# Loading every second chunk of Q with an outer dimension of 8 in a grouped-query attention kernel

## The chip, the cores and the metric

The kernel runs on one core of a Trainium2 chip. The metric is the device time of one execution in microseconds (us). "PE" is the matrix engine, "DVE" the vector engine, "ACT" the scalar engine, "POOL" the GpSimd engine and "SP" the sync engine, which issues nearly all DMA transfers here. A transfer from memory (HBM) into on-chip memory (SBUF, 128 partitions) is moved in packets (37349 in the kernel before) by sixteen DMA engines side by side: each K load shows sixteen arrivals, near 20 us within 0.44 us. Profiles are of one execution; times are medians of several executions without the profiler. Kernels are compared only within the same rounds.

## The reference

```python
B, Hq, Hkv, Sq, Sk, D = 16, 32, 8, 16, 2048, 128      # all bfloat16

def reference(q, k, v):
    k = jnp.repeat(k, Hq // Hkv, axis=1)               # four query heads share one K/V head
    v = jnp.repeat(v, Hq // Hkv, axis=1)
    scores = jnp.einsum("bhqd,bhkd->bhqk", q, k) * D ** -0.5
    p = softmax(scores, axis=-1)
    return jnp.einsum("bhqk,bhkd->bhqd", p, v)
```

K and V hold 67 MB each and are read once; Q and the output hold 2.1 MB each. In the profile, 136.3 MB are read from memory and 2.1 MB written.

## The kernel before

One queue (SP) loads K and V in pieces of 1 MB into a ring of fifteen buffers ("slots"), and Q in eight chunks of 1024 rows, 256 KB each. A slot is loaded again as soon as the work that read it is done. Each chunk of Q is rearranged on POOL (the first on DVE and ACT), transposed on PE, and read out of PSUM in the right row order by ACT or DVE. A Q row has 256 bytes; NI is 8, so a partition gets eight neighbouring rows.

```python
for t in range(NP + LAG):                 # order of issue on the one queue
    if t < NP:             dma.append(("K", t))
    if qstep.get(t, 0):    dma.append(("Q", qstep[t]))
    if t >= LAG:           dma += v_of(t - LAG)
    ...                                   # and the output stores

# the load of chunk x of Q: partition a gets rows 8a to 8a+7
dst, src = Qn[x % 2][:, :, :], qf[qch * x:qch * (x + 1), :].rearrange("(a i) d -> a i d", i=NI)
sp.dma_start(dst, src).then_inc(*prog_sem(prog, op))        # its semaphore counts to 16

# "qt": eight transposes of 128 x 128, one for each i
for i in range(NI):
    pe.transpose(QT_ps[:, 128 * i:128 * (i + 1)], Qr[:, x, i, :], ident[:, :])

# "qe": the PSUM read, which puts the rows back into order
dst = QT[p % 2][:, op[2], :].rearrange("d (a i) -> d a i", i=NI)
src = QT_ps[:, 0:qch].rearrange("d (i a) -> d a i", i=NI)
```

A 1 MB load of K or V fills all 128 partitions with 8 KB each, K in packets of 8 KB and V (all but its last, halved piece) in packets of 4 KB. An output store reads 64 partitions.

Of the kernel before, what the change touches and what calls it, by code (L numbers as in the profile page):

```python
# [210 lines left out]
def bass_standalone__gqa_softmax__sampling_kernel(  # L211
# [14 lines left out]
    qch = min(QCH, NROWS)  # L226
    assert NROWS % qch == 0 and qch % 128 == 0
    NI = qch // 128
# [8 lines left out]
    Qn = [sb(f"Qn{i}", [128, NI, 128], BF16) for i in range(2)]  # L237
    Qr = sb("Qr", [128, 4, NI, 128], BF16)
    QT = [sb(f"QT{i}", [128, 4, qch], BF16) for i in range(2)]
# [19 lines left out]
    QT_ps = ps("QT_ps", [128, 1024], BF16)  # L259
# [58 lines left out]
    qf = q.rearrange("b h s d -> (b h s) d")  # L318
# [6 lines left out]
    def mark_hint(eng, me, prog, op):  # L325

        if not prog.general and op == prog.progs[me][max(0, len(prog.progs[me]) - HINT[me])]:
            hints[me] = eng.mark_branch_hint_location()

    def o_tile(p):  # L330
        return Osb[(p // 2 if p < NP - 1 else NP // 2) % NBO][:, p % 2, :]

    def out_rows(p, gg):

        g = group_of(p, gg)
        return of[64 * g:64 * (g + 1), :], o_tile(p)[64 * gg:64 * (gg + 1), :]

    def prog_sem(prog, op):
        return prog.point(op)[0], 16

    def group_of(p, gg):
        return 4 * (p // 2) + 2 * gg + p % 2

    def elementwise(eng, me, prog, before_last=None):
        waits = prog.waiter(eng, me)
        for op in prog.progs[me]:
            kind, p = op[0], op[1]
            if before_last is not None and op == prog.progs[me][-1]:
                before_last()
            waits(op)  # L350
            mark_hint(eng, me, prog, op)
            if kind == "kx":
                _, _, gg, h = op
                ins = eng.transpose(KT[p % NKT][:, gg, :, h],  # L354
                                    prog.slot(("K", 2 * p + gg))[:, J * 64 * h:J * 64 * (h + 1)])
            elif kind == "qr":
                x = op[2]
                dst = Qr[:, x, :, :].rearrange("m i (a d) -> m i a d", a=4)
                src = bass.AP(Qn[p % 2], (x // 2) * 64 + x % 2, [[NI * 128, 128], [128, NI], [0, 4], [2, 32]])
                ins = eng.activation(dst, src, ACT.Copy) if me == "act" else eng.tensor_copy(dst, src)  # L360
            elif kind == "mx":
                h, part = op[2], slice(Sk // 2 * (p % 2), Sk // 2 * (p % 2 + 1))
                ins = eng.tensor_scalar(Sneg[p % 2][:, Sk // 2 * h:Sk // 2 * (h + 1)], S_ps[:, part], -scale, None,
                                        op0=ALU.mult, op1=ALU.min, accum_out=nhalf[:, p, h:h + 1])
            elif kind == "nb":
                ins = eng.tensor_tensor(nbias[:, p:p + 1], nhalf[:, p, 0:1], nhalf[:, p, 1:2], op=ALU.min)
            elif kind == "ex":
                h = op[2]
                if prog.general:
                    src = Sneg[p % 2][:, Sk // 2 * h:Sk // 2 * (h + 1)]  # L370
                else:
                    src = S_ps[:, Sk // 2 * (p % 2):Sk // 2 * (p % 2 + 1)]
                ins = eng.activation(  # L373
                    P[p % 2][:, :].rearrange("m (r a h j) -> m h a r j", h=2, a=2, j=32)[:, h],
                    src.rearrange("m (a r j) -> m a r j", a=2, j=32), ACT.Exp,
                    bias=nbias[:, p:p + 1] if prog.general else 0.0, scale=-1.0 if prog.general else scale,
                    accum_out=rhalf[:, p, h:h + 1])
            elif kind == "rs":
                ins = eng.tensor_tensor(rowsum[:, p:p + 1], rhalf[:, p, 0:1], rhalf[:, p, 1:2], op=ALU.add)  # L379
            elif kind == "STA":  # L380
                eng.dma_start(*out_rows(NP - 1, 1)).then_inc(*prog_sem(prog, op))
                continue
            elif kind == "rc":
                ins = eng.reciprocal(rrec[:, p:p + 1], rowsum[:, p:p + 1])  # L384
            elif kind == "nm":
                dst, src, r = o_tile(p), O_ps[:, 0:128], rrec[:, p:p + 1]
                if me == "act":
                    ins = eng.activation(dst, src, ACT.Copy, scale=r)  # L388
                else:
                    ins = eng.tensor_scalar(dst, src, r, None, op0=ALU.mult)  # L390
            else:
                if kind == "qe":
                    dst = QT[p % 2][:, op[2], :].rearrange("d (a i) -> d a i", i=NI)
                    src = QT_ps[:, 0:qch].rearrange("d (i a) -> d a i", i=NI)
                else:
                    h = op[2]
                    dst = PT[p % NPT][:, 8 * h:8 * (h + 1), :]
                    src = PT_ps[h][:, :].rearrange("k (t m) -> k t m", t=8)
                ins = eng.activation(dst, src, ACT.Copy) if me == "act" else eng.tensor_copy(dst, src)  # L399
            ins.then_inc(prog.sem_eng[me], 1)  # L400

    def transfers(sp, prog):
        waits = prog.waiter(sp, "sp")
        for op in prog.progs["sp"]:
            kind, x = op
            waits(op)
            mark_hint(sp, "sp", prog, op)
            if kind == "K":
                dst = prog.slot(op)[:, :].bitcast(BF16)
                src = kf[2 * x:2 * x + 2].rearrange("g (b r) d -> (g b) (r d)", r=2 * J)  # L410
            elif kind[0] == "V":
                p, part = (x, slice(0, J)) if kind == "V" else (NP - 1, slice(J // 2 * x, J // 2 * (x + 1)))
                g = group_of(p, 0)
                dst = prog.v_rows(p)[:, :, part, :].rearrange("a g r d -> a g (r d)")
                src = vf[g:g + 3:2].rearrange("g (a r) d -> a g r d", r=J)[:, :, part, :].rearrange("a g r d -> a g (r d)")
            elif kind == "Q":
                dst, src = Qn[x % 2][:, :, :], qf[qch * x:qch * (x + 1), :].rearrange("(a i) d -> a i d", i=NI)
            elif x >= NP // 2 - 1:
                p = NP - 2 if x == NP // 2 - 1 else NP - 1
                for gg in range(2 if p == NP - 2 else 1):  # L420
                    sp.dma_start(*out_rows(p, gg)).then_inc(*prog_sem(prog, op))
                continue
            else:
                for gg in range(2):
                    g = 4 * x + 2 * gg
                    sp.dma_start(of[64 * g:64 * (g + 2), :].rearrange("(p m) d -> m p d", p=2),
                                 Osb[x % NBO][64 * gg:64 * (gg + 1), :, :]).then_inc(*prog_sem(prog, op))
                continue
            sp.dma_start(dst, src).then_inc(*prog_sem(prog, op))
# [62 lines left out]
    with nc.Block() as block:  # L492

        @block.gpsimd
        def _(gp):
            gp.iota(iota_t[:, :], [[1, 128]], base=0, channel_multiplier=-1).then_inc(sem_id, 1)
            gp.memset(ones[:, :], 1.0).then_inc(sem_id, 1)
            gp.wait_ge(sem_id, 2)
            gp.tensor_scalar(ident[:, :], iota_t[:, :], 0.0, None, op0=ALU.is_equal).then_inc(sem_id, 1)
            elementwise(gp, "pool", fast)  # L500
            unless_in_range(gp, "pool", lambda: elementwise(gp, "pool", general))

        @block.sync
        def _(sp):
            transfers(sp, fast)

            def again():
                transfers(sp, general)
                general.wait_stores(sp)

            unless_in_range(sp, "sp", again)
            fast.wait_stores(sp)
# [54 lines left out]
```

## Time and profile before

| | before |
|---|---|
| time, median of the first three runs | 348.36 us (348.19 to 348.55) |
| span of the profile | 346.9 us |
| bytes moved, mean rate | 139.21 MB, 401 GB/s |
| PE, DVE, ACT busy | 69%, 65%, 65% of the span |
| chain of waits | 72% K loads |

The lines below are from the profile's page for the kernel before. "DMA" is the mean busy share of the sixteen DMA engines, in tenths, in forty equal slices of the span; "GB/s" is what they moved in each slice. The line with q8 is a queue that fetches instructions: packets, MB, share of sixteen engines. Then comes the chain of work that ended last, by engine. The lines with L399 are the PSUM reads of Q (count, then busy us and mean ns of one, then the idle time before them); the last two are DMA issues (count, KB each, median us from issue to landing).

```profile
span 346.9 us, 11937 instructions
...
DMA  7999999999999999999999999999999999999983
GB/s 309 426 412 415 411 413 412 412 415 414 411 418 415 412 412 414 415 413 414 413 412 417 414 415 414 414 413 415 413 413 414 412 417 416 414 412 412 392 336 108
DMA packets 37349, 139.21 MB, mean 401 GB/s; under 512 B 11440, under 2 KB 11440, under 8 KB 29104
...
q8 instruction: 43, 0.70, 0.8%
...
DMA 72%; DVE 11%; PE 9%; ACT 6%; issue 1%; SPq 0%; ACTq 0%
...
L399 ACT ACTIVATE QT<-QT_ps 128x1024 bf16<-128x1024 bf16 x23 | 23.5, 1023 | 7.3 <-PE QT_ps L440 7.3
...
L399 DVE COPY QT<-QT_ps 128x1024 bf16<-128x1024 bf16 x9 | 10.9, 1209 | 1.8 <-PE QT_ps L440 1.8
...
slot<-in_k_dram SPq DMA_DIRECT2D x64, 1024.0 KB, 17.6
...
Qn<-in_q_dram SPq DMA_DIRECT2D x8, 256.0 KB, 15.3
```

The rate is flat at about 414 GB/s from the second slice to the thirty-seventh. The engines are hardly without work in that stretch (their busy share is 1.02 to 1.03 in windows of 40 us from 40 to 320 us), so I take it that a transfer is as fast as the engines go through their packets. In the packet records an 8 KB packet takes 309 ns (median), a 4 KB packet of V 159 ns and a 2 KB packet of Q 84 ns.

The semaphore records show sixteen separate arrivals for each plain load. The records name no engine; I take each arrival as the moment when one engine's share has landed. Here are the arrivals of one late V load in the kernel before, as lags in us behind the first, sorted:

```
before, first at 312.7 us:
0.0 0.1 0.2 0.2 0.4 0.9 1.8 2.7   6.0 6.2 7.7 7.9 7.9 7.9 8.1 8.2
```

Near 20 us all sixteen are still within 0.44 us. Eight engines then fall behind, each by about 1.5 us beside one of the 43 fetches of instructions (16 KB, median 1.07 us). The first fetch starts at 23.0 us; of the load whose arrivals begin at 23.9 us the last one, at 25.92 us, is 1.6 us behind the fifteenth. I call those eight the laden engines and the other eight the free ones. What needs a load waits for its last arrival: a K load's arrivals run from 310.2 to 318.34 us, and its transpose on DVE starts at 318.37 us. So the laden engines set the pace.

Which eight they are can be read from the output stores, although the records name no engine. A store from partitions 0 to 63, issued right behind this V load, lands from 312.9 to 315.8 us, with its sixteen arrivals in pairs at the lags of the first eight engines. The store from partitions 64 to 127 lands from 318.9 to 321.3 us, with the last eight. So the free engines serve the stores from partitions 0 to 63.

### The profile page before, as it was taken

What the parts mean: (1) busy time and instruction counts of PE and PEld (TensorE: products, weight loads), DVE (VectorE), ACT (ScalarE), POOL (GpSimd) and SP (SyncE); (2) the same over time, 40 slices, a digit from 0 to 9 for tenths busy, and PEclk for the clock granted to TensorE, in tenths of its full rate; (3) what the DMA queues carried; (4) which work ended last, traced back from release to release, by engine and by line L of the source; (5) the groups of instructions that cost most, each with busy time, mean ns of one, the idle gap of its engine ahead of it and who ended that gap; (6) DMA issues with size and microseconds to landing.
All of it is one profiled execution on the core that took longest, in us unless ns stands there. A gap on an engine that the chain in (4) does not pass through costs nothing.

```text
span 346.9 us, 11937 instructions
## 1 busy us (share of the span) xinstructions
PE 238.6 (69%) x5378; PEld 172.7 (50%) x5378; DVE 225.8 (65%) x377; ACT 226.6 (65%) x369; POOL 29.0 (8%) x35
## 2 busy tenths in 40 slices
PE   1568868756686668766687665865857757576785
PEld 1345646534464446543465453643645545454564
DVE  4867996874775666746666655767559476576544
ACT  4496887665586575946759646787558746477551
POOL 1310031000400004000040000400004000000000
PEclk9998999999899898999989989999899989899899
DMA  7999999999999999999999999999999999999983
GB/s 309 426 412 415 411 413 412 412 415 414 411 418 415 412 412 414 415 413 414 413 412 417 414 415 414 414 413 415 413 413 414 412 417 416 414 412 412 392 336 108
DMA packets 37349, 139.21 MB, mean 401 GB/s; under 512 B 11440, under 2 KB 11440, under 8 KB 29104
## 3 DMA queue, kind: packets, MB, share of 16 engines
q1 hardware_dynamic: 37216, 138.41, 98.9%
q8 instruction: 43, 0.70, 0.8%
q14 instruction: 10, 0.08, 0.1%
q10 hardware_dynamic: 80, 0.02, 0.0%
HBM read 136.31 MB, written 2.10 MB: 399 GB/s over the span
## 4 chain that ended last, share of the span: by engine, by line
DMA 72%; DVE 11%; PE 9%; ACT 6%; issue 1%; SPq 0%; ACTq 0%
DMA slot<-in_k_dram 72%; DVE KT L354 9%; PE O_ps L468 3%; ACT P L373 2%; PE PT_ps L462 2%; PE S_ps L452 2%; PE QT_ps L440 1%; ACT QT L399 1%; DVE PT L399 1%; ACT PT L399 1%; DMA Qn<-in_q_dram 1%; DVE O L390 1%; ACT L360 0%; ACT Qr L360 0%; DVE rowsum L379 0%
## 5 line engine op out<-in xcount | busy, mean ns | idle before, releaser
L354 DVE STREAM_TRANSPOSE KT<-slot 128x1024 int32<-128x1024 int32 x128 | 154.5, 1231 | 101.3 <-DMA slot<-in_k_dram 92.8
L373 ACT ACTIVATE P<-S_ps 128x1024 bf16<-128x1024 f32 x128 | 130.5, 1025 | 87.5 <-PE PT_ps L462 49.6
L462 PE MATMUL PT_ps<-ident,P 128*128 128x128 bf16 x1024 | 74.4, 229 | 83.1 <-DVE PT L399 44.0
L462 PEld LDWEIGHTS PT_ps<-ident,P 128*128 128x128 bf16 x1024 | 62.3, 102 | 104.7 <-DVE PT L399 53.7
L452 PE MATMUL S_ps<-KT,QT 32*64 32x512 bf16 x2048 | 75.9, 401 | 11.0 <-ACT P L373 9.7
L468 PE MATMUL O_ps<-slot,PT 128*64 128x128 bf16 x2048 | 76.7, 233 | 1.3 <-DVE O L390 1.0
L468 PEld LDWEIGHTS O_ps<-slot,PT 128*64 128x64 bf16 x2048 | 65.9, 119 | 17.8 <-issue 14.2
L399 ACT ACTIVATE PT<-PT_ps 128x1024 bf16<-128x1024 bf16 x60 | 61.1, 1019 | 3.0 <-PE PT_ps L462 2.1
L360 POOL COPY Qr<-Qn 128x1024 bf16<-128x1024 bf16 x28 | 28.0, 1042 | 235.2 <-DMA Qn<-in_q_dram 235.2
L399 DVE COPY PT<-PT_ps 128x1024 bf16<-128x1024 bf16 x68 | 45.2, 668 | 1.8 <-PE PT_ps L462 1.8
L452 PEld LDWEIGHTS S_ps<-KT,QT 32*64 32x64 bf16 x2048 | 28.1, 106 | 32.3 <-ACT P L373 12.9
L440 PE MATMUL QT_ps<-ident,Qr 128*128 128x128 bf16 x256 | 22.1, 236 | 10.2 <-ACT Qr L360 6.1
L399 ACT ACTIVATE QT<-QT_ps 128x1024 bf16<-128x1024 bf16 x23 | 23.5, 1023 | 7.3 <-PE QT_ps L440 7.3
L373 ACT ACTIVATION_READ_ACCUMULATOR P<-S_ps 128x1 f32 x128 | 25.9, 202 | 0.0
L440 PEld LDWEIGHTS QT_ps<-ident,Qr 128*128 128x128 bf16 x256 | 16.7, 105 | 16.5 <-issue 8.3
L388 ACT ACTIVATE O<-O_ps,rrec 128x128 bf16<-128x128 f32 x27 | 9.9, 367 | 11.6 <-PE O_ps L468 11.6
L390 DVE TENSOR_SCALAR O<-O_ps,rrec 128x128 bf16<-128x128 f32 x37 | 12.0, 324 | 5.5 <-PE O_ps L468 5.4
L399 DVE COPY QT<-QT_ps 128x1024 bf16<-128x1024 bf16 x9 | 10.9, 1209 | 1.8 <-PE QT_ps L440 1.8
L379 DVE TENSOR_TENSOR rowsum<-rhalf 128x1 f32<-128x1 f32 x64 | 8.5, 152 | 4.4 <-ACT P L373 4.4
L384 DVE RECIPROCAL rrec<-rowsum 128x1 f32<-128x1 f32 x64 | 8.5, 153 | 0.5
L360 ACT ACT_TABLE_LOAD x1 | 1.3, 1283 | 3.6 <-DMA Qn<-in_q_dram 3.6
L360 DVE COPY Qr<-Qn 128x1024 bf16<-128x1024 bf16 x2 | 1.3, 690 | 3.5 <-DMA Qn<-in_q_dram 3.5
(13 smaller groups left out, 4.2 us busy)
## 6 DMA issues: line engine op xcount, KB each, us to landing
slot<-in_k_dram SPq DMA_DIRECT2D x64, 1024.0 KB, 17.6
slot<-in_v_dram SPq DMA_DIRECT2D x63, 1024.0 KB, 17.7
Qn<-in_q_dram SPq DMA_DIRECT2D x8, 256.0 KB, 15.3
out_dram<-O SPq DMA_DIRECT2D x62, 32.0 KB, 13.2
slot<-in_v_dram SPq DMA_DIRECT2D x2, 512.0 KB, 12.3
out_dram<-O SPq DMA_DIRECT2D x3, 16.0 KB, 1.8
out_dram<-O ACTq DMA_DIRECT2D x1, 16.0 KB, 2.0
```

Source lines behind the costliest of these rows:

```text
L354: ins = eng.transpose(KT[p % NKT][:, gg, :, h], prog.slot(("K", 2 * p + gg))[:, J * 64 * h:J * 64 * (h + 1)])
L360: ins = eng.activation(dst, src, ACT.Copy) if me == "act" else eng.tensor_copy(dst, src)
L373: ins = eng.activation(P[p % 2][:, :].rearrange("m (r a h j) -> m h a r j", h=2, a=2, j=32)[:, h], src.rearrange("m (a r j) -> m a r j", a ...
L379: ins = eng.tensor_tensor(rowsum[:, p:p + 1], rhalf[:, p, 0:1], rhalf[:, p, 1:2], op=ALU.add)
L384: ins = eng.reciprocal(rrec[:, p:p + 1], rowsum[:, p:p + 1])
L388: ins = eng.activation(dst, src, ACT.Copy, scale=r)
L390: ins = eng.tensor_scalar(dst, src, r, None, op0=ALU.mult)
L399: ins = eng.activation(dst, src, ACT.Copy) if me == "act" else eng.tensor_copy(dst, src)
L440: ins = pe.transpose(QT_ps[:, 128 * i:128 * (i + 1)], Qr[:, x, i, :], ident[:, :],)
L452: ins = pe.matmul(S_ps[64 * gg:64 * (gg + 1), 512 * a:512 * (a + 1)], QT[c % 2][32 * a:32 * (a + 1), x, row:row + 64], kt[:, :, x // 2, p ...
L462: ins = pe.transpose(PT_ps[h][:, 128 * t:128 * (t + 1)], P[p % 2][:, 128 * r:128 * (r + 1)], ident[:, :])
L468: ins = pe.matmul(O_ps[64 * gg:64 * (gg + 1), 0:128], PT[p % NPT][:, r, 64 * gg:64 * (gg + 1)], prog.v_rows(p)[:, gg, r, :], start=(r == 0 ...
```

## The change

The intent was to take work off the eight laden engines. With an outer dimension of 8 on the side of memory, every second chunk of Q (1, 3, 5, 7) should use eight engines only. The rows then land in another order: partition 16x + y gets the eight rows that start at row 8(8y + x) of the chunk. The PSUM read undoes this.

```diff
+    def few_engines(c):
+
+        return c % 2 == 1
+
...
                 if kind == "qe":
-                    dst = QT[p % 2][:, op[2], :].rearrange("d (a i) -> d a i", i=NI)
-                    src = QT_ps[:, 0:qch].rearrange("d (i a) -> d a i", i=NI)
+                    if few_engines(p):
+                        dst = QT[p % 2][:, op[2], :].rearrange("d (y x i) -> d y x i", x=8, i=NI)
+                        src = QT_ps[:, 0:qch].rearrange("d (i x y) -> d y x i", i=NI, x=8)
+                    else:
+                        dst = QT[p % 2][:, op[2], :].rearrange("d (a i) -> d a i", i=NI)
+                        src = QT_ps[:, 0:qch].rearrange("d (i a) -> d a i", i=NI)
...
             elif kind == "Q":
-                dst, src = Qn[x % 2][:, :, :], qf[qch * x:qch * (x + 1), :].rearrange("(a i) d -> a i d", i=NI)
+                dst, src = Qn[x % 2][:, :, :].rearrange("a i d -> a (i d)"), qf[qch * x:qch * (x + 1), :]
+                if few_engines(x):
+                    src = src.rearrange("(y x i) d -> x y (i d)", x=8, i=NI)
+                else:
+                    src = src.rearrange("(a i) d -> a (i d)", i=NI)
```

## The prediction

> **What bounds the kernel now.** The DMA engines. The page has DMA at 9 tenths in nearly every slice, at about 414 GB/s; the compute engines are 65 to 69% busy. The chain of waits is 72% K loads, 17.5 to 19 us from issue to landing, so several megabytes are always queued. In the packet records an 8 KB packet takes 309 ns and the next follows at once: each engine runs at a fixed pace (1 MB per 2.5 us over all), and a load is there only when its slowest engine is done.
>
> The engines are not equally loaded. I took the sixteen semaphore arrivals of every load. Near 20 us they are within 0.44 us. Then one engine after another falls back by about 1.5 us, beside one of the 43 instruction fetches of 16 KB (queue q8, about 1.05 us each). Eight engines take them in turn. At the last K load (323 us) eight engines arrive within 2.8 us and the other eight 6.0 to 8.2 us after the first. Output stores tell which: one from partitions 0 to 63 lands wholly with the fast eight, one from 64 to 127 with the slow eight. [...]
>
> **What the change does.** [...] No trace so far shows k = 8.
> - Removed from each slow engine: 4 x 8 packets of 2 KB. One takes 80 ns from start to start, with the semaphore 0.65 us per chunk: 2.6 us in all.
> - Added to each fast engine: the same 2.6 us.
> - Bytes, descriptors, instructions and schedule stay.
> - The 16 changed PSUM reads keep 1024 elements and contiguous writes; I expect 1.02 us on ACT and 1.21 us on DVE as now, off the chain.
>
> **How much is on the critical path.** All 2.6 us, if the mapping is so: the slow engines are never without work until the last V halves (last landing 343.3 us, 3.6 us before the end), and later loads wait for their landings. The lags become 2.6 to 5.4 us for the fast group and 3.4 to 5.6 us for the slow: nearly balanced. The tail after the last K load moves with it. So 348.4 - 2.6, less a little at the start, where the fast engines are briefly the later ones.
>
> **Predicted: 346.0 us**, range 345.1 to 349.0. Faster by over 2%: 1%; within 2%: 96%; slower by over 2%: 3%.
>
> **What would show it.** The spread of the arrivals of late K loads falls from 8.2 to about 3 us; the two groups merge. Span about 344.4 us; packet durations and Q copies unchanged; K loads still head the chain.
>
> **What would make it wrong.** The engines. The 64-partition stores put two shares on each of eight engines chosen by partition, so k = 8 might follow partitions too. If four of the slow group get extra work, 2.6 us are lost (351); if two of them get double shares, 7.8 us (356); if all sixteen share it, nothing changes. A compute-bound tail could also swallow part of the gain.

Here k is the number of engines that a load uses. The assumption is that chunks 1, 3, 5 and 7 go to the eight fast engines alone. 348.4 - 2.6 = 345.8 us, with some 0.2 us put back for the start, came to the 346.0 us predicted. But the whole 2.6 us rest on that assumption.

## The result, and the profile after

Ratios here and below are the mean time of one kernel's fast runs over that of the other's of the same rounds, so they are not quite the ratio of the medians beside them. The brackets hold the 95% interval.

| | before | after |
|---|---|---|
| time, median of five runs each | 348.36 us | 357.34 us (356.88 to 358.56) |
| ratio | | 1.0262 [1.0240, 1.0283] |
| span of the profile | 346.9 us | 355.1 us |
| mean granted clock of PE | 0.944 | 0.946 |

The change made the kernel slower by 2.6%, or 9 us. The prediction was a gain of 2.4 us, with a range up to 349.0. The lines of the page after the change that answer to those above:

```profile
span 355.1 us, 11937 instructions
...
DMA  7999999999999999999999999999999999999992
GB/s 305 366 417 413 413 412 411 413 413 416 337 416 417 413 412 415 413 415 413 374 359 414 416 417 410 415 415 415 407 349 386 414 413 412 417 416 404 388 350 61
DMA packets 37318, 139.22 MB, mean 392 GB/s; under 512 B 11408, under 2 KB 11408, under 8 KB 29072
...
q8 instruction: 43, 0.70, 0.8%
...
DMA 71%; DVE 12%; PE 10%; ACT 5%; issue 1%; ACTq 0%
...
L407 ACT ACTIVATE QT<-QT_ps 128x1024 bf16<-128x1024 bf16 x23 | 23.5, 1023 | 20.1 <-PE QT_ps L452 20.1
...
L407 DVE COPY QT<-QT_ps 128x1024 bf16<-128x1024 bf16 x9 | 10.9, 1209 | 3.0 <-PE QT_ps L452 3.0
...
slot<-in_k_dram SPq DMA_DIRECT2D x64, 1024.0 KB, 17.9
...
Qn<-in_q_dram SPq DMA_DIRECT2D x8, 256.0 KB, 16.1
```

Much is as predicted. The PSUM reads still take 1023 and 1209 ns, and the chain of waits is still 71% DMA. The packets under 512 B are 32 fewer (11440 before, 11408 after). That is eight packets of 4 bytes for each of four chunks (3232 such packets on the queue of the loads before, 3200 after), which I take for the engines' semaphore writes. The semaphore records say so, too: for chunk 1, issued at 3.10 us, one update came at 4.27 us, long before any of its data, and eight more between 15.65 and 16.3 us. In the kernel before, the sixteen arrivals of chunk 1 came between 13.93 and 14.36 us. So the odd chunks do run on eight engines.

What is new are four dips in the line of GB/s, in slices 2, 11, 20 and 21, and 30 and 31. The "DMA" line does not show them: the engines are busy at nine tenths or more while they move less. The next two fences are the profile's table of windows around the odd chunks, first of before, then of after. The columns are the window, its length, busy us and count of PE, weight loads, DVE, ACT and POOL, the granted clock of PE, the DMA engines' busy share, and GB/s.

```profile
11.50:15.50 4.00, 1.62 (x24) 1.22 (x32) 3.88 (x4) 2.05 (x2) 1.09 (x2) 1.00 1.02 424
86.50:92.50 6.00, 3.43 (x56) 3.07 (x52) 4.18 (x9) 2.59 (x5) 0.62 (x1) 0.76 1.02 416
170.50:177.00 6.50, 4.16 (x90) 3.52 (x80) 4.83 (x10) 3.15 (x5) 0.60 (x1) 0.84 1.03 415
253.00:261.50 8.50, 5.83 (x152) 4.46 (x160) 4.82 (x10) 4.96 (x11) 0.61 (x1) 1.00 1.02 409
```

```profile
12.50:16.50 4.00, 2.60 (x40) 1.44 (x40) 3.12 (x4) 1.07 (x2) 0.12 (x1) 1.00 1.02 289
88.50:96.50 8.00, 3.21 (x80) 2.24 (x80) 3.92 (x7) 4.42 (x8) 0.56 (x1) 1.00 1.02 329
172.50:183.50 11.00, 6.29 (x160) 4.45 (x160) 6.13 (x11) 7.40 (x13) 0.51 (x1) 1.00 1.03 337
258.00:270.00 12.00, 7.81 (x196) 4.98 (x192) 6.90 (x12) 8.97 (x16) 0.00 (x0) 0.97 1.02 345
```

The busy share is 1.02 or 1.03 in all eight lines, and the rate falls from some 415 to between 289 and 345 GB/s. Against 414 GB/s, the windows of after lose 4.00 x (1 - 289/414) = 1.2 us, then 1.6, 2.0 and 2.0 us: 6.9 us in all. The same sum over the windows of before is zero within 0.1 us. So 6.9 of the 9 us are lost while an odd chunk is in flight (the spans of the two profiled executions differ by a little less, 8.2 us), and they are lost as packets that take longer. Between 13.5 and 15.0 us after the change the median 2 KB packet takes 152 ns and the median 8 KB packet 538 ns; in the same stretch before (13.0 to 14.5 us) they take 84 and 309 ns. The records do not name a packet's engine, but for most of this stretch sixteen or more slow packets are under way at once, so the engines that carry nothing of Q are slow as well.

Some 1.3 to 2 us remain. The arrivals of the late V load point at them:

```
after, first at 319.5 us:
0.0 0.0 2.7 3.1 3.3 3.6 3.7 3.8 3.8 4.4 4.7 5.0 5.1 5.5   10.2 10.3
```

If the eight free engines had taken the load, two groups of eight should have come close together. Instead fourteen engines lie within 5.5 us of the first, and two are 10 us late.

The stores tell who these two are. The store from partitions 0 to 63 behind this load (from 319.7 us) has four updates within 0.2 us and twelve that are 2.7 to 3.9 us later: two of the eight free engines carry no odd chunk, six do. The store from partitions 64 to 127 (from 323.6 us) has its last four updates 6.2 to 6.6 us after its first, when the two late engines arrive: two of the laden engines carry the odd chunks.

### The profile page after: what moved, and what is told of

Read it like the earlier page. It is cut to its first block, busy times and chain, and to the rows that moved or that the text cites. A ratio compares the mean times of both kernels' runs of the same rounds, so it can differ in the third digit from the quotient of the medians.

```text
span 355.1 us, 11937 instructions
## 1 busy us (share of the span) xinstructions
PE 239.9 (68%) x5378; PEld 171.8 (48%) x5378; DVE 226.7 (64%) x377; ACT 226.8 (64%) x369; POOL 29.0 (8%) x35
## 2 busy tenths in 40 slices
DMA packets 37318, 139.22 MB, mean 392 GB/s; under 512 B 11408, under 2 KB 11408, under 8 KB 29072
## 4 chain that ended last, share of the span: by engine, by line
DMA 71%; DVE 12%; PE 10%; ACT 5%; issue 1%; ACTq 0%
DMA slot<-in_k_dram 71%; DVE KT L358 9%; PE PT_ps L474 3%; PE O_ps L480 2%; ACT P L377 2%; PE S_ps L464 2%; DVE PT L407 2%; ACT QT L407 1%; PE QT_ps L452 1%; ACT PT L407 1%; DMA Qn<-in_q_dram 1%; DVE O L394 1%; ACT L364 0%; ACT Qr L364 0%; DVE rowsum L383 0%
## 5 line engine op out<-in xcount | busy, mean ns | idle before, releaser
L474 PE MATMUL PT_ps<-ident,P 128*128 128x128 bf16 x1024 | 73.2, 227 | 77.7 <-DVE PT L407 47.3
L474 PEld LDWEIGHTS PT_ps<-ident,P 128*128 128x128 bf16 x1024 | 61.3, 101 | 99.0 <-DVE PT L407 47.1
L464 PE MATMUL S_ps<-KT,QT 32*64 32x512 bf16 x2048 | 77.9, 413 | 11.1 <-ACT P L377 9.9
L480 PE MATMUL O_ps<-slot,PT 128*64 128x128 bf16 x2048 | 74.7, 230 | 1.0 <-DVE O L394 1.0
L480 PEld LDWEIGHTS O_ps<-slot,PT 128*64 128x64 bf16 x2048 | 64.1, 116 | 17.9 <-issue 13.2
L364 POOL COPY Qr<-Qn 128x1024 bf16<-128x1024 bf16 x28 | 28.0, 1042 | 244.3 <-DMA Qn<-in_q_dram 244.3
L452 PE MATMUL QT_ps<-ident,Qr 128*128 128x128 bf16 x256 | 24.2, 250 | 22.7 <-POOL Qr L364 11.3
L407 ACT ACTIVATE QT<-QT_ps 128x1024 bf16<-128x1024 bf16 x23 | 23.5, 1023 | 20.1 <-PE QT_ps L452 20.1
L452 PEld LDWEIGHTS QT_ps<-ident,Qr 128*128 128x128 bf16 x256 | 18.3, 112 | 29.7 <-POOL Qr L364 16.8
L407 DVE COPY QT<-QT_ps 128x1024 bf16<-128x1024 bf16 x9 | 10.9, 1209 | 3.0 <-PE QT_ps L452 3.0
```

What stands on the lines that cost most here:

```text
L364: ins = eng.activation(dst, src, ACT.Copy) if me == "act" else eng.tensor_copy(dst, src)
L407: ins = eng.activation(dst, src, ACT.Copy) if me == "act" else eng.tensor_copy(dst, src)
L452: ins = pe.transpose(QT_ps[:, 128 * i:128 * (i + 1)], Qr[:, x, i, :], ident[:, :],)
L464: ins = pe.matmul(S_ps[64 * gg:64 * (gg + 1), 512 * a:512 * (a + 1)], QT[c % 2][32 * a:32 * (a + 1), x, row:row + 64], kt[:, :, x // 2, p ...
L474: ins = pe.transpose(PT_ps[h][:, 128 * t:128 * (t + 1)], P[p % 2][:, 128 * r:128 * (r + 1)], ident[:, :])
L480: ins = pe.matmul(O_ps[64 * gg:64 * (gg + 1), 0:128], PT[p % NPT][:, r, 64 * gg:64 * (gg + 1)], prog.v_rows(p)[:, gg, r, :], start=(r == 0 ...
```

## The experiments

There were two questions. Why do all packets slow down while an odd chunk is in flight? And what becomes of the relief of the laden engines without that slowdown?

**1. The order in memory, the reading, and the count of engines.** Three theories were on record before this set. PORTS: each of the eight engines writes partitions that other engines write in a plain load, and they wait on each other. HBM: the changed load reads interleaved rows of memory, and that is slow. EIGHT: any load on eight engines unbalances the queues. The changed PSUM read was a further rival. None of these was shown by a trace so far. Four kernels went together.

The first keeps eight engines, but gives each engine a run of memory of its own (with overlaps, so the rows are wrong). The second keeps the plain split over sixteen engines, but reads rows 16 KB apart (wrong rows, too). The third takes 16 in place of 8 everywhere. The fourth has the changed PSUM read alone (wrong rows).

```diff
 # first, against the kernel after; the PSUM read is that of before
-                    src = src.rearrange("(y x i) d -> x y (i d)", x=8, i=NI)
+                    src = bass.AP(q.tensor, q.offset + qch * x * D, [[120 * D, 8], [NI * D, 16], [1, NI * D]])
 # second; the PSUM read is that of before
-                    src = src.rearrange("(y x i) d -> x y (i d)", x=8, i=NI)
+                    src = bass.AP(q.tensor, q.offset + x * NI * D, [[8 * NI * D, 128], [1, NI * D]])
 # third: x=16 for x=8 in the load and in the PSUM read
 # fourth: the load of before, the PSUM read of after
```

> Odd Q chunks still on k = 8, but each of the eight shares reads one contiguous 32 KB stretch of HBM, not 2 KB pieces 16 KB apart (rows of odd chunks are wrong on purpose). Theory PORTS (each of the eight engines writes 16 neighbouring partitions[...], and all wait on each other): as slow as the change, 355 to 359 us, DMA dips to about 250 GB/s near 14, 91, 177 and 262 us. Theory HBM (the strided reads are slow): dips gone, about 346 us. Theory EIGHT (any transfer on eight engines unbalances the queues): 355 to 359 us.

> Odd Q chunks on all sixteen engines with the plain split over 128 partitions, but every partition reads its 2 KB from HBM 16 KB away from its neighbour's (wrong rows on purpose). PORTS: no change, 348 to 349 us. HBM: dips appear, 350 to 357 us. EIGHT: 348 to 349 us.

> As the change, but with an outer dimension of 16 (8 partitions for each share): sixteen engines, rows permuted and put right, right results. PORTS: if a share is eight neighbouring partitions, [...] shorter dips, 349 to 352 us; if the shares are the plain ones, 348.4 us. HBM: dips, 350 to 357 us. EIGHT: 348 to 349 us.

> Only the other part of the change: the permuted PSUM read of the odd chunks, with the loads as before (wrong rows on purpose). All theories: 348 to 349 us, Q copies 1.02 us on ACT and 1.21 us on DVE as before.

Measured, against before in the same rounds (median 348.29 us of seven runs):

| kernel | median us (four runs) | ratio |
|---|---|---|
| first: own run of memory, eight engines | 357.85 | 1.0282 [1.0258, 1.0305] |
| second: rows 16 KB apart, plain split | 348.89 | 1.0015 [0.9999, 1.0032] |
| third: outer dimension 16 | 353.58 | 1.0151 [1.0126, 1.0176] |
| fourth: PSUM read alone | 348.29 | 1.0000 [0.9983, 1.0016] |

The lines of GB/s of the first, the second and the third, in this order:

```profile
GB/s 311 368 415 414 415 408 415 409 416 414 337 417 415 414 416 411 416 414 416 372 358 413 419 415 411 413 418 411 408 343 386 418 412 412 416 415 409 388 362 68
```

```profile
GB/s 313 408 420 416 411 414 411 410 416 413 413 416 415 416 411 414 415 413 411 414 413 416 414 415 414 413 417 414 412 416 416 413 416 414 415 416 413 380 349 116
```

```profile
GB/s 308 395 418 414 410 410 415 413 414 413 349 416 415 414 414 410 417 414 411 382 378 417 414 413 413 415 414 414 417 362 396 412 416 415 415 416 411 390 336 106
```

The order in memory is not the cause: with a run of memory for each engine the dips are all there, and with rows far apart there are none. The PSUM read costs nothing. And an outer dimension of 8 is not needed for a dip: the third kernel, with 16, dips (5.3 us slower, a little above the 349 to 352 us that PORTS gave). Its lags are those of before (latest 8.3 us behind the first), so here the slowdown of packets stands alone, without a shift of work between engines.

What the slow loads share is how the 128 partitions are cut: into eight or sixteen blocks, where the loads without dips have an outer dimension of 128. PORTS is the one theory left. It was not shown: no record names the engine or the partition of a packet. I call the slowdown a collision from here on, whatever causes it.

**2. Odd chunks in the lower 64 partitions.** If the destination counts, a load into partitions 0 to 63 alone should use the free engines at full speed. That was an estimate from the stores: a store from partitions 0 to 63 lands wholly with the first eight arrivals (312.9 to 315.8 us in the kernel before). A chunk then has sixteen rows on each of 64 partitions. This needs one larger Q buffer in place of two; the first kernel of this set has that buffer and nothing else. The second and the third load the odd chunks to 64 partitions with an outer dimension of 64 and of 8, and leave the rest (wrong rows). The fourth is the second with sixteen transposes of 64 rows and a PSUM read that fits, for right results. The cuts below show the main lines only.

```diff
 # first (one buffer), against before
-        add(("Q", c), *[opt(c >= 2, ("qr", c - 2, x)) for x in range(4)])
+        add(("Q", c), *[opt(c >= 1, ("qr", c - 1, x)) for x in range(4)])
-    Qn = [sb(f"Qn{i}", [128, NI, 128], BF16) for i in range(2)]
+    Qn = sb("Qn", [128, 2 * NI, 128], BF16)
 # second, against the first
+                if x % 2 == 1:
+                    dst = Qn[0:64, :, :].rearrange("a i d -> a (i d)")
+                    src = qf[qch * x:qch * (x + 1), :].rearrange("(a i) d -> a (i d)", i=2 * NI)
 # third: the same dst, and
+                    src = bass.AP(q.tensor, q.offset + qch * x * D, [[120 * D, 8], [2 * NI * D, 8], [1, 2 * NI * D]])
 # fourth: the load of the second, and for odd chunks
+                n, m = (2 * NI, 64) if p % 2 else (NI, 128)      # n transposes of m rows
```

> Control for the next three: the kernel before with one Q buffer of twice the size in place of two (room for rows of 4 KB); loads and PSUM reads as before, right results. All theories: 348 to 349 us.

> Odd Q chunks go to partitions 0 to 63 alone, 4 KB each, with the plain split of a 64-partition transfer (wrong rows on purpose). The stores show that such a transfer uses the eight engines of the lower half[...]. PORTS: no dips; the slow eight engines lose 2.6 us of work, 345.5 to 346.5 us, spread of late K loads 3 to 4 us. EIGHT: half of the engines carry the chunk as in the change, so 355 to 359 us. HBM is out by now.

> The same bytes into the same 64 partitions on the same eight engines, but through an outer dimension of 8[...] (wrong rows on purpose). PORTS: dips come back, now for the eight engines of the lower half alone; packets of the upper eight keep 309 ns; the lower half becomes the late one; 350 to 357 us. Without PORTS: as the run before, near 346 us.

> The aim of the change without its collision, with right results: odd Q chunks in partitions 0 to 63 with 16 rows each, transposed in 16 blocks of 64 rows, put in order by the PSUM read. PORTS: as with wrong rows, 345.5 to 346.8 us, faster than both kernels by about 0.7% and 3%. EIGHT: 355 us or more.

Measured, against before in the same rounds (median 348.58 us of nine runs):

| kernel | median us (five runs) | ratio |
|---|---|---|
| first: one Q buffer | 348.42 | 1.0004 [0.9990, 1.0017] |
| second: 64 partitions, outer 64 | 355.90 | 1.0217 [1.0201, 1.0233] |
| third: 64 partitions, outer 8 | 357.29 | 1.0253 [1.0237, 1.0269] |
| fourth: as the second, right results | 354.76 | 1.0195 [1.0171, 1.0218] |

The line of GB/s of the second:

```profile
GB/s 312 386 418 413 410 413 413 411 414 415 343 414 415 413 417 415 408 417 414 364 339 415 415 416 414 411 417 417 411 361 388 415 415 415 414 416 412 388 339 96
```

The one buffer costs nothing. The expected 346 us of the second and the fourth failed, because a *load* to 64 partitions is not split as a *store* from 64 partitions is. Chunk 1 landed with sixteen arrivals between 14.66 and 15.18 us, four packets of 4 KB each: all sixteen engines took part. The dips came as in the changed kernel (343, 364, 339 and 361 GB/s in the worst slices). The sixteen engines carry equal shares here and the lags stay at 8.4 us, so the 7.3 us of the second kernel are the slowdown of packets alone. In the third (expected 350 to 357 us, measured 357.29), sixteen slow packets were under way at once, K packets of 420 to 600 ns among them, so I take it that the engines without Q were slow as well; I had expected them to stay at full speed.

**3. A probe of shapes.** To stop guessing, I put groups of loads in front of the program's own transfers, each group waited for before the next. In the first half four loads of one shape go alone; in the second half one load of 256 KB goes between two K loads on either side. The program's own time then says nothing (561 us); the packet records are what counts.

```diff
+            for kind in kinds:
+                go(*[small(kind, n if kind[0] == "q" else n // 2, n) for n in range(4)])
+            for kind in kinds:
+                go(big(4, 0), big(5, 1), small(kind, 0, 0), big(6, 2), big(7, 3))
```

> The kernel before with a probe in front of it, right results, some 150 us longer, its time says nothing. Ten shapes of a 256 KB load of Q rows, each first four times alone and waited for, then once between K loads of 1 MB (two before, two after): the plain one of 128 partitions; the permuted ones with outer dimension 8 (the change), 16 and 32; 64 partitions, lower and upper half, plain, and lower half with outer dimension 8; 32 partitions with outer dimension 8 at partition 0 and at 64, and 32 partitions plain. PORTS[...]: [...] 32 partitions with outer dimension 8 at partition 0 [...] keeps full speed alone and beside K loads, while the same at partition 64 does not beside K loads. GLOBAL (any split but the plain one slows all engines, whatever it writes): all shapes but the plain one are slow, the one at partition 0 too. MIXED ONLY (it takes K loads beside it): all shapes fast alone, slow only between K loads.

Measured, durations of packets in ns; "p90" is the ninth tenth:

| shape of the load of 256 KB | beside K loads | alone |
|---|---|---|
| plain, 128 partitions | 2 KB median 84, 8 KB median 309 | 2 KB median 84 |
| outer 8, 128 partitions (the change) | 2 KB median 152, p90 178; 8 KB p90 548 | 2 KB median 84 |
| outer 16, 128 partitions | 2 KB p90 136 | 2 KB median 124 |
| outer 32, 128 partitions | 2 KB median 84, 8 KB median 309 | 2 KB median 84 |
| outer 64, partitions 0 to 63 | 4 KB p90 373 | 4 KB median 309 |
| outer 64, partitions 64 to 127 | 4 KB p90 340 | 4 KB median 313 |
| outer 8, partitions 0 to 63 | 8 KB p90 497 | 4 KB median 160 |
| outer 32, partitions 0 to 31 (plain) | 8 KB p90 551 | 8 KB median 636 |
| outer 8, partitions 0 to 31 | 8 KB p90 312 | 8 KB median 309 |
| outer 8, partitions 64 to 95 | 8 KB p90 590 | 8 KB median 309 |

This table shows that the place counts. Beside K loads, outer 8 at partitions 0 to 31 runs at full speed (8 KB p90 312 ns); the same load at partitions 64 to 95 is slow (8 KB p90 590 ns). Outer 32 over all partitions runs at full speed (84 and 309 ns), which speaks against GLOBAL. And the change's own load alone is at full speed (84 ns), as is the load at 64 (309 ns): they are slow only with the K loads beside them. The plain loads to 32 or 64 partitions are at half speed even alone: 636 ns against 309, and 309 or 313 against 159 for the 4 KB packet.

One thing stays unexplained: alone, the load of outer 8 to partitions 0 to 63 ran at full speed (160 ns), and the load of outer 64 to the same partitions at half (309 ns). What makes the difference no run here shows.

I had expected that only some of the engines would slow down. That is not so: beside the load at 64 sixteen slow packets were under way at once, with a median of 616 ns for 8 KB.

**4. Full speed, with right results.** Now the odd chunks can be loaded without a collision: in two loads with an outer dimension of 8, one into partitions 0 to 31, which the probe showed at full speed, and one into partitions 32 to 63. That the second would be at full speed, too, was the estimate; no run had shown it. The transposes are those of the fourth kernel of set 2, with a PSUM read for the new order (it and the count of the semaphore are not shown below). With it went two loads of 128 KB with wrong rows that differ in one number, the first partition.

```diff
 # first (right results): against the fourth kernel of set 2
+                    src = qf[qch * x:qch * (x + 1), :].rearrange("(y h x i) d -> h x y (i d)", h=2, x=8, i=2 * NI)
+                    for h in range(2):
+                        dst = Qn[32 * h:32 * (h + 1), :, :].rearrange("a i d -> a (i d)")
+                        sp.dma_start(dst, src[h]).then_inc(*prog_sem(prog, op))
 # second (wrong rows): against the one-buffer kernel; third: Qn[64:96]
+                    dst = Qn[0:32, :, :].rearrange("a i d -> a (i d)")
+                    src = bass.AP(q.tensor, q.offset + qch * x * D, [[120 * D, 8], [2 * NI * D, 4], [1, 2 * NI * D]])
```

> The aim of the change with right results and no collision: an odd Q chunk goes to partitions 0 to 31 and 32 to 63 in two loads, each with outer dimension 8[...], which the probe showed at full speed for 0 to 31. PORTS: no dips, the slow eight engines lose 2.6 us, spread of late K loads 3 to 4 us, 345.5 to 346.8 us, the fastest of all. GLOBAL (already unlikely after the probe): dips, 354 us or more.

> In the kernel: half of an odd Q chunk (128 KB, wrong rows on purpose) into partitions 0 to 31 with outer dimension 8. The eight fast engines then carry as much Q as before, the slow eight none. PORTS: no dips, 345 to 346.5 us. GLOBAL: dips, 352 us or more.

> As the run before in all but the first partition, 64 in place of 0: same bytes, same shape, same HBM rows. PORTS: [...] while a Q chunk is in flight all packets take about twice their time (8 KB: about 616 ns, as in the probe); dips, 349 to 354 us. If engines followed the partitions instead: no dips, 348 to 349 us. GLOBAL: as at partition 0.

Measured, against before in the same rounds (median 348.64 us of eleven runs):

| kernel | median us | ratio |
|---|---|---|
| first: two loads, partitions 0 to 63, right results | 351.04 (six runs) | 1.0056 [1.0027, 1.0085] |
| second: outer 8 at partition 0, 128 KB | 347.64 (four runs) | 0.9969 [0.9942, 0.9997] |
| third: outer 8 at partition 64, 128 KB | 352.71 (four runs) | 1.0117 [1.0093, 1.0142] |

The windows of the first around its odd chunks, with the columns as above:

```profile
12.50:16.50 4.00, 2.61 (x40) 1.44 (x40) 3.85 (x4) 1.06 (x2) 1.11 (x1) 1.00 1.01 426
88.00:96.00 8.00, 5.77 (x105) 4.67 (x106) 5.16 (x8) 3.99 (x8) 3.35 (x2) 0.79 1.02 412
171.00:178.00 7.00, 5.76 (x157) 4.13 (x154) 5.36 (x10) 4.68 (x9) 0.45 (x1) 1.00 1.03 417
254.50:263.00 8.50, 6.25 (x160) 4.49 (x160) 5.22 (x10) 6.12 (x11) 0.39 (x1) 1.00 1.02 407
```

The lines of GB/s of the second and the third:

```profile
GB/s 311 428 413 416 411 412 413 411 415 414 414 415 414 415 415 414 413 416 415 413 414 414 415 416 413 416 415 412 416 416 414 413 414 414 415 415 403 385 352 85
```

```profile
GB/s 314 393 415 414 413 410 415 412 414 415 357 417 416 414 414 416 413 415 412 372 388 417 415 417 413 416 414 415 417 367 394 413 417 414 414 414 404 385 352 86
```

The dips are gone with two loads at partitions 0 to 63 (407 to 426 GB/s in the windows) and with one at partition 0, and there at 64 (357, 372, 367 GB/s in the worst slices): moving the same load by 64 partitions costs 352.71 - 347.64 = 5.1 us. The arrivals of both are spread alike (10.0 us), so only the slowdown differs. That settles the first question as far as the kernel is concerned.

But the first kernel, which does what the change intended and without the dips, takes 351.04 us where I expected 346. Its arrivals are these:

```
two loads of outer 8, right results, first at 312.7 us:
0.0 0.5 2.0 2.5 2.9 3.6 3.7 3.9 5.0 5.1 5.1 5.2 5.2 5.2   9.9 10.0
```

It is the picture of the changed kernel again: fourteen engines close together, two late by 10 us. The stores behind this load say the same as above: the one from partitions 64 to 127 (from 317.8 us) has its last four updates 4.9 to 5.2 us after its first. Two of the laden engines are among the eight that take the odd chunks. They get more work, not less (2.6 us by the prediction's costing), and every load waits for them. The second kernel, too, stayed above its expected 345 to 346.5 us: its last two arrivals are 9.8 and 10.0 us behind the first. One caution: this kernel also does more on POOL (a rearranging copy of 64 partitions takes 1889 ns, against 1042 before), and DMA is only 54% of its chain of waits. So its 2.4 us over before need not be those two engines alone.

**5. Fewer engines.** With the wrong-row loads of set 4 in two halves, an outer dimension of 4 uses four engines and one of 6 uses six (4 and 6 updates come from each such load, after one early one); each engine used then gets 32 KB of an odd chunk, double its plain share of 16 KB, and the others get none. The second probe asks how many engines slow down when loads of outer dimension 2, 4 or 8 start at other partitions. In the expectations, SET is the case that no laden engine is among those used. "Own" partitions are those from 0 and from 32, "others'" those from 8, 16 and 64: from estimates, for no record names an engine's partitions.

```diff
 # outer 4, against the one-buffer kernel; outer 6: 24 for 16 and 6 for 4
+                    for h in range(2):
+                        dst = Qn[32 * h:32 * h + 16, :, :].rearrange("a i d -> a (i d)")
+                        src = bass.AP(q.tensor, q.offset + qch * x * D, [[120 * D, 4], [2 * NI * D, 4], [1, 2 * NI * D]])
+                        sp.dma_start(dst, src).then_inc(*prog_sem(prog, op))
 # the second probe: outer k, first partition as given, two such loads between K loads
+            for kind in ("k2_0", "k2_8", "k2_64", "k4_0", "k4_16", "k4_64", "k8_0", "k8_32", "k8_64"):
+                go(big(8, 0), big(9, 1), *[small(kind, n, n) for n in range(2)], big(10, 2), big(11, 3))
```

> Odd Q chunks (half the bytes, wrong rows on purpose) in two loads with outer dimension 4 into partitions 0 to 15 and 32 to 47: four engines, 32 KB each a chunk in place of 16 KB[...]. SET [...]: no dips, all engines with fetches lose 2.6 us, 345.3 to 346.5 us, spread of late K loads near 5 us. If one with fetches is among the four: it gains 2.6 us, 350 to 352 us. If relieving does not count at all: 348 to 349 us.

> The same with outer dimension 6 (24 partitions a load, 192 KB a chunk, wrong rows on purpose): six engines with 32 KB each. SET, with the two engines with fetches as the last two of the eight: as with four, 345.3 to 346.5 us. With one of them among the first six: 350 to 352 us, spread above 10 us.

> A second probe in front of the kernel before (time says nothing): loads with outer dimension 2, 4 and 8 (four partitions an engine, two loads each) between K loads, at the engines' own partitions (from 0; 8 at 32 too) and at others' (from 8 or 16, from 64). LOCAL: at the own ones all packets keep 309 ns; at others' about twice as many engines as load Q have packets of about 616 ns, four with outer dimension 2, eight with 4, sixteen with 8, the others keep 309. GLOBAL: all sixteen slow in each wrong place.

Measured, against before in the same rounds (median 348.47 us of eleven runs):

| kernel | median us | ratio |
|---|---|---|
| outer 4 (wrong rows) | 345.62 (six runs) | 0.9918 [0.9901, 0.9936] |
| outer 6 (wrong rows) | 350.37 (five runs) | 1.0052 [1.0036, 1.0067] |

```
outer 4, first at 309.6 us:
0.0 0.3 0.5 1.1   5.2 5.5 6.3 6.6 7.6 7.9 8.1 8.2 8.2 8.3 8.3 8.3
outer 6, first at 313.1 us:
0.0 0.2 0.5 1.8 1.8 2.9 3.1 3.2 3.3 3.9 4.5 4.6 4.6 4.8 4.8   9.9
```

The four engines of outer 4 are all free ones: the store from partitions 0 to 63 shows the four that carry more, and the one from 64 to 127 lands within 1.0 us, with no straggler. All laden engines are relieved, and the kernel gains 2.85 us. (It also moves 128 KB less for each odd chunk, 0.5 MB in all, which at 414 GB/s would be 1.3 us. The second kernel of set 4 moves as many bytes less and gains 1.0 us, with an interval of the ratio that lies clear of this one's. So some 1.8 us of the gain go with the choice of engines.) I had expected the spread of the arrivals to fall to about 5 us, and it stayed at 8.3. The first arrival moved from 312.7 to 309.6 us: free engines that carry nothing of these chunks were relieved, too, so the front of the field moved ahead with the rear. With six engines one is late by 9.9 us, and two updates of the store from 64 to 127 are as late: one of the six is laden. With eight, two are (last arrivals at 9.8 and 10.0 us in the second kernel of set 4).

The second probe's windows, in the order of the list in its edit; only the last column matters. Then the packets: where the rate is halved, the median slow packet of 8 KB took 619 to 648 ns in all five cases, and where it is full none in these windows took over 309 ns.

```profile
6.50:10.00 3.50, 0.00 (x0) 0.00 (x0) 0.00 (x0) 0.00 (x0) 0.00 (x0) 1.00 1.02 431
22.50:27.40 4.90, 0.00 (x0) 0.00 (x0) 0.00 (x0) 0.00 (x0) 0.00 (x0) 1.00 0.99 219
39.50:44.30 4.80, 0.00 (x0) 0.00 (x0) 0.00 (x0) 0.00 (x0) 0.00 (x0) 1.00 0.99 210
55.00:60.00 5.00, 0.00 (x0) 0.00 (x0) 0.00 (x0) 0.00 (x0) 0.00 (x0) 1.00 1.00 421
71.00:75.60 4.60, 0.00 (x0) 0.00 (x0) 0.00 (x0) 0.00 (x0) 0.00 (x0) 1.00 0.98 216
87.80:92.60 4.80, 0.00 (x0) 0.00 (x0) 0.00 (x0) 0.00 (x0) 0.00 (x0) 1.00 1.00 222
103.50:108.50 5.00, 0.00 (x0) 0.00 (x0) 0.00 (x0) 0.00 (x0) 0.00 (x0) 1.00 1.00 423
118.50:123.50 5.00, 0.00 (x0) 0.00 (x0) 0.00 (x0) 0.00 (x0) 0.00 (x0) 1.00 1.02 429
134.00:139.50 5.50, 0.00 (x0) 0.00 (x0) 0.00 (x0) 0.00 (x0) 0.00 (x0) 1.00 0.99 235
```

Outer 2 at partition 0: 431 GB/s. The same at partition 8 or at 64: 219 and 210. Outer 4 at 0: 421; at 16 or 64: 216 and 222. Outer 8 at 0 or at 32: 423 and 429; at 64: 235. In every slow case the median number of slow packets under way at once was sixteen. So the expectation that only some of the engines slow down (LOCAL) fell a second time: even with outer 2 at partition 8 or 64 the rate of all the traffic is halved.

**What the numbers say of right results.** The comparison with the reference cannot tell the order of the rows within its tolerance (with inputs this small the softmax is nearly flat). That the changed kernel and the kernel of 351.04 us put the rows right rests on the index arithmetic alone.

**A version that beats both?** The one with outer dimension 4 does, by 0.8%, but with wrong rows and half of each odd chunk left out. With all rows, the bytes that twelve engines lose go to four: if u us are taken off each of the twelve, each of the four gets 3u. The latest engine is then at 8.2 - u, or at 2.8 + 3u if that is more, so the best u is about 1.35 us, or 0.4% of the time. This is an estimate from the lags shown above. It needs 32 rows on each of 32 partitions, 8 KB each, where the two buffers of Q now have 4 KB together; whether that fits beside fifteen slots was not tried. I did not build it.

## Why the prediction was wrong

Point by point, in the order of the prediction:

- **"The DMA engines bound the kernel"**: right. The chain of waits stayed at 71%, and in the kernels whose late arrivals were read, the latest engine's arrival moved with the time, though not to the microsecond. For the same late V load, against before (312.7 + 8.2 = 320.9 us); arrival and span are of one profiled execution each, so these two belong together:

| kernel | latest arrival | against before | span against before (346.9) | time against before (medians of the same rounds) |
|---|---|---|---|---|
| after | 329.8 | +8.9 | +8.2 | +9.0 |
| two loads of outer 8, right results | 322.7 | +1.8 | +3.3 | +2.4 |
| outer 6 | 323.0 | +2.1 | +0.8 | +1.9 |
| outer 8 at partition 0, 128 KB | 320.6 | -0.3 | -1.1 | -1.0 |
| outer 4 | 317.9 | -3.0 | -3.1 | -2.85 |

- **Eight engines for four of the eight chunks** (assumed): right. Eight semaphore writes fewer for each odd chunk, and the one early update, show it.
- **The PSUM reads**: right, 1023 and 1209 ns as before, and the read alone costs nothing (348.29 us on both sides).
- **"Packet durations unchanged"**: wrong, and this is the step that made the kernel slow. While an odd chunk is in flight, packets take about 1.75 times as long (538 against 309 ns for 8 KB), with sixteen or more slow ones under way at once for most of the stretch read. The windows show 6.9 us lost. The kernel of two loads, which has the same aim without the collision, measured 357.34 - 351.04 = 6.3 us less (7.2 us by the ratios, 1.0262 and 1.0056). I had costed the load as the same packets on other engines, and had not asked where those engines write.
- **The eight engines without fetches** (assumed): wrong. Of the eight engines that take the odd chunks, two are laden, as the late updates of the stores from partitions 64 to 127 show. I had taken the engines from the stores: those from partitions 0 to 63 land with the free engines. But a store is split otherwise than a load here: a store from 64 partitions lands in pairs, at the lags of eight engines, and a load to 64 partitions (second kernel of set 2) landed with sixteen arrivals within 0.52 us. The two laden engines get 2.6 us more instead of 2.6 us less, by the prediction's own costing of a share. In the kernel without dips that is 351.0 expected from 348.4 + 2.6, and 351.04 measured; the close match is partly luck, for the ratio makes it +2.0 us, the latest arrival +1.8, and the runs go from 349.55 to 352.32.
- **"2.6 us removed from each slow engine", all of it on the critical path**: about right where all laden engines are really relieved. With four free engines it measured 348.47 - 345.62 = 2.85 us, and the latest arrival moved by 3.0; but that kernel also moves 0.5 MB less, so the term is not measured by itself.
- **The arrivals' spread of about 3 us**: wrong. It was 10.3 us, for the reason just given.
- **"What would make it wrong: the engines"**: the right place, but I put the wrong sizes to it (351 if four laden engines got extra work) and did not think of a slowdown of all engines at all. That its other case, 356 us for double shares on two laden engines, lies near the measured 357.34 is luck: two laden engines did get more, but by the costing only 2.6 us, and the rest is the slowdown.

The sum is 348.4 + 2.0 to 2.6 (two late engines: the ratio of the kernel without dips, and the costing) + 6.9 (collisions, by the windows) = 357.3 to 357.9 us, against 357.34 measured.

What stays open is the mechanism of the collision. In the probes, with loads of 64 KB to 256 KB beside K loads, the slowdown came with outer 8 and 16 over 128 partitions, with outer 64 and 8 on 64 partitions, with outer 32 on partitions 0 to 31, with outer 2 from partition 8 or 64, outer 4 from 16 or 64, and outer 8 from 64 (210 to 235 GB/s in the second probe). It did not come with the plain load, with outer 32 over 128 partitions, or with outer 2, 4 or 8 from partition 0 and outer 8 from 32 (421 to 431 GB/s). Where it was worst, sixteen slow packets were under way at once, those of 8 KB at some 620 ns in place of 309, more than the outer dimensions of 2, 4 or 8 of the loads of Q. That an engine disturbs the others when it writes partitions that they write in the K loads is only a reading of these results; no trace names the engine or the partition of a packet.

## What to carry to other kernels

When a transfer is moved to other engines, ask two things: which engines, by the trace of such a transfer itself and not by that of another kind (here stores from 64 partitions landed in pairs, at the lags of eight engines, and a load to 64 partitions with sixteen arrivals), and whether the new place slows the transfers beside it (here the same load cost 5.1 us more at partition 64 than at 0). The "busy" line did not show the collision (1.02 or 1.03 with and without it); the line of GB/s (289 to 345 in place of some 415) and the durations of single packets (538 in place of 309 ns) did. Test a new shape of load next to the traffic that it will meet: alone, the change's own load ran at full speed (84 ns a packet of 2 KB), and beside K loads it took 152 ns.
